# Sparse attention and a gated MLP on one core: scores on row halves, selection by added mask matmuls, and an engine order written out as a table

## The chip, the cores and the metric

One core of one Trainium2 chip runs the whole program. The metric is the device time of one execution in microseconds (us), lower is better; the profile's span, from the first to the last instruction, lies a few microseconds below it. TensorE is called PE here, VectorE DVE, ScalarE ACT, GpSimd POOL, SyncE SP.

## What is computed

For 4 batches and 8 heads, with 768 positions and head size 64, every query may look at its 6 best chunks of 32 keys. The choice goes by an upper bound of the chunk's scores:

```python
k_min, k_max = min and max over each chunk of 32 keys        # 24 chunks
ub = sum(maximum(q * k_min, q * k_max))                      # a bound for each query and chunk
ub = where(query's chunk >= chunk, ub, -1e9)
sel = the 6 chunks with the largest ub
scores = where(sel and causal, q k^T / 8, -1e9)
x = softmax(scores) @ v                                      # heads side by side: 768 x 512 per batch
h = gelu(x @ w_in);  u, v = halves of h
v = layernorm(v) * g_ln;  v = w_sg @ v + b_sg                # a 768 x 768 matrix over the positions
out = x + (u * v) @ w_out
```

Queries of the first 192 positions have at most 6 chunks and need no choice; the bounds concern the other 576.

## The kernel before

The program is made as a list of operations, each with an engine, a cost, the data that it reads and writes, and a priority. `schedule` places them by a greedy list schedule at build time; each engine then runs its own list in order, and semaphores hold what crosses engines. `fill` puts idle matmuls on a zero tile (L463) into early gaps of PE. Operations marked `port` on DVE are kept, in that schedule, out of the time of POOL's operations. Loads go by SP with at most 4 in flight. PSUM has two score tiles of 128x1024 (PSC) and four tiles of 128x512 (PSG), of which two (slots 2 and 3) serve the MLP.

Work goes by pairs of heads (16 pairs, two heads on partitions 0 to 63 and 64 to 127), and the selection by two pairs together (8 groups):

- `kside`: PE transposes k in f32 (L540), DVE takes the minimum and maximum of each chunk out of PSUM (`W`, L546, L559), ACT copies k in bf16 to `KA` and `KB` (L551 for pairs 0 to 3, L555 after).
- `qside`: the same for q (L575), ACT evacuates it to `qT` (L580), DVE makes `rT`, its positive part (L584), POOL casts it to `QA` (L587, L589, L592). From pair 4 on, DMAs on SP move the second head's half to `KB` and `QB`.
- `select`: for each half of the 576 queries, 8 f32 matmuls of 64 rows x 32 columns (L613; each shows as two instructions), DVE transposes the result to `U` (L621), takes the 8 largest of 18 query blocks (L629), compares (`Dn`, L632), and transposes back: eight transposes of 32x576 straight into `QA` and `QB` for pairs 0 to 3 (L640), one into `Dt` and DMAs after that (L644).
- `head`: the score matmul of one head has the selection in its contraction. `KA` and `KB` hold 64 rows of k and 24 or 64 rows of chunk indicators, `QA` and `QB` hold q and the selection. So one head is 14 bf16 matmuls with 2688 columns in all (L677), in three PSC tiles of 1024, 1024 and 640 columns, each followed by one exp on ACT (L682). POOL zeroes the upper triangles (L686), 21 matmuls of 65 columns make the output (L696, L703), DVE normalizes it (L711, L713).
- `xtrans`: PE transposes x (L723), DVE evacuates it (L727). `wsg_trans` does the same for w_sg (L735, L739).
- `moe_h(b)`: 24 matmuls of 512 columns for v (L751), gelu, statistics (L758, L760), the root on POOL (L764), six normalizations on DVE (L767), and 32 matmuls of 384 columns for u (L777). `moe_g(b)`: 48 matmuls of 384 columns (L794), two DVE operations each for the gate (L801, L805), 24 matmuls of 512 columns (L814), the residual (L820), the store.

The weights come by DMAs on POOL's queue that cast on the way (L498, L503, L508), issued after heads 0 to 6.

Of the kernel before, what the change touches and what calls it, by code (L numbers as in the profile page):

```python
# [13 lines left out]
LAT = {"pe": 0.15, "act": 0.20, "dve": 0.12, "pool": 0.15, "sp": 0.05}  # L14
TABLE_SWITCH = 1.3
WINDOW = 4


class PsumTile:


    def __init__(self, cls, slots=None):
        self.cls = cls
        self.slots = slots
        self.left = 0
        self.slot = None
        self.end = 0.0
        self.ops = []
# [6 lines left out]
class PsumClass:  # L35
    def __init__(self, aps):
        self.aps = aps
        self.owner = [None] * len(aps)

    def tile(self, slots=None):  # L40
        return PsumTile(self, slots)


class Op:
    __slots__ = ("eng", "fn", "cost", "prio", "deps", "dma", "ps", "alloc", "table", "burst",
                 "start", "end", "pos", "waits", "inc", "count", "idx", "lane", "bulk", "port")


class Program:

# [3 lines left out]
    def __init__(self):  # L54
        self.ops = []
        self.writer = {}
        self.readers = {}
        self.dma_sems = {}
        self.base = 0.0

    def op(self, eng, fn, cost, reads=(), writes=(), ps=(), alloc=None, dma=None, table=None,
           burst=None, prio=None, lane=0, bulk=False, port=False):
        o = Op()
        o.bulk = bulk
        o.port = port or (eng == "pool" and dma is None)
        o.lane = lane
        o.idx = len(self.ops)
        o.eng, o.fn, o.cost, o.dma, o.table, o.burst = eng, fn, cost, dma, table, burst
        o.prio = (self.base if prio is None else prio) + 1e-4 * o.idx
        deps = {}  # L70
        ps = tuple(ps) + ((alloc,) if alloc is not None else ())
        o.ps, o.alloc = ps, alloc
        for t in ps:
            t.left += 1
            for x in reversed(t.ops):
                if x.eng != eng:
                    deps.setdefault(x.idx, False)
                    break
            t.ops.append(o)
        for r in reads:  # L80
            w = self.writer.get(r)
            if w is not None:
                deps[w] = True
        for r in writes:
            w = self.writer.get(r)
            if w is not None:
                deps[w] = True
            for x in self.readers.get(r, ()):
                deps.setdefault(x, False)
# [5 lines left out]
        if dma is not None:  # L95
            last = self.dma_sems.setdefault(dma, [])
            if last:
                deps[last[-1]] = True
            last.append(o.idx)
        o.deps = deps  # L100
# [3 lines left out]
    def schedule(self):  # L104
        ops = self.ops
        succ = [[] for _ in ops]
        ndep = [len(o.deps) for o in ops]
        alloc = {o.alloc: o for o in ops if o.alloc is not None}
        for o in ops:
            hold = set()  # L110
            for t in o.ps:
                a = alloc[t]
                if a is not o:
                    hold.update((d, a.idx) for d in o.deps if d < a.idx and d not in a.deps)
            for d, a in hold:
                if a not in succ[d]:
                    succ[d].append(a)
                    ndep[a] += 1
            for d in o.deps:
                succ[d].append(o.idx)  # L120
        ready = {e: [] for e in ENGINES}
        rt = [0.0] * len(ops)
        for o in ops:
            if ndep[o.idx] == 0:
                ready[o.eng].append(o.idx)
        free = {e: 0.0 for e in ENGINES}
        order = {e: [] for e in ENGINES}
        table = None
        burst_left = {}
        for o in ops:  # L130
            if o.burst is not None:
                burst_left[o.burst] = burst_left.get(o.burst, 0) + 1
        cur_burst = None
        pool_owner = {}

        def slot_for(t, now):
            best = None
            for i, own in enumerate(t.cls.owner):
                if t.slots is not None and i not in t.slots:
                    continue  # L140
                at = 0.0 if own is None else (own.end if own.left == 0 else None)
                if at is not None and (best is None or at < best[0]):
                    best = (at, i)
            return best

        n = 0
        dma_free = 0.0
        soft_free = 0.0
        flight = []
        held = {"pool": 0.0, "dve": 0.0}  # L150
        while n < len(ops):
            pick = None
            for e in ENGINES:
                cands = []
                for i in ready[e]:
                    o = ops[i]
                    t = max(rt[i], free[e])
                    if o.alloc is not None and o.alloc.slot is None:
                        s = slot_for(o.alloc, t)
                        if s is None:  # L160
                            continue
                        t = max(t, s[0] + 0.15)
                    if e == "act" and o.table is not None:
                        if cur_burst is not None and o.burst != cur_burst:
                            continue
                        if o.table != table:
                            t += 0.0
                    if o.port:
                        t = max(t, held["pool" if e == "dve" else "dve"])
                    if o.bulk and len(flight) >= WINDOW:  # L170
                        t = max(t, ops[flight[-WINDOW]].end)
                    cands.append((t, o.prio, i))
                if not cands:
                    continue
                tmin = min(c[0] for c in cands)
                best = min((c for c in cands if c[0] <= tmin + 0.02), key=lambda c: c[1])
                if pick is None or best[0] < pick[0]:
                    pick = (best[0], e, best[2])
            if pick is None:
                raise RuntimeError("no operation can be scheduled")  # L180
            t, e, i = pick
            o = ops[i]
            ready[e].remove(i)
            if o.alloc is not None and o.alloc.slot is None:
                at, s = slot_for(o.alloc, t)
                old = o.alloc.cls.owner[s]
                if old is not None:
                    for x in old.users:
                        o.deps.setdefault(x, False)
                o.alloc.slot = s  # L190
# [13 lines left out]
            if o.port:  # L204
                held[e] = t + cost
# [703 lines left out]
```

## Time and profile before

| | |
|---|---|
| time, median of 3 runs | 267.15 us (265.14 to 267.54) |
| span of the profiled execution | 262.9 us |
| mean granted clock of PE, as a share of 2.4 GHz | 0.968 |
| DVE, ACT, POOL busy | 197.7, 153.4, 76.9 us |
| HBM read, written | 24.77 MB, 6.29 MB |

The table of runs gives no time of its own for the profiled execution; 262.9 us of span stand 4.25 us below the median. A busy PE is not a PE at its peak: matmuls are pipelined, and the recorded time of a group goes on past the start of the next. How long a group holds PE is read from the start of the next one where nothing is waited for.

### The profile page before, as it was taken

The numbers are of one execution on the slowest core, as the hardware profiler recorded it, in microseconds if no ns is written. First come the engines' busy times: TensorE is split into PE (matmuls) and PEld (weight loads), VectorE is DVE, ScalarE is ACT, GpSimd is POOL, SyncE is SP. The second block draws the span as 40 slices with busy tenths as digits, with TensorE's granted clock in tenths as the row PEclk, the third lists the DMA queues.
The fourth block names the chain that finished last, engine by engine and source line by source line (L and its number), as shares of the span: only waits on it lengthen the run. The fifth ranks groups of instructions, "written<-read, shape, count | busy, mean of one in ns | idle before, by whom it ended". The sixth has DMA issues, their size and how long they took to land.

```text
span 262.9 us, 5801 instructions
## 1 busy us (share of the span) xinstructions
PE 225.0 (86%) x2242; PEld 140.2 (53%) x2258; DVE 197.7 (75%) x561; ACT 153.4 (58%) x232; POOL 76.9 (29%) x99
## 2 busy tenths in 40 slices
PE   8886488987996599998899899997998998689874
PEld 3444256665743378655555577566445765434431
DVE  6949579787558668989677988886588876467883
ACT  1444848977649545655784974658757645846000
POOL 3353728653201424222212433134210211202000
PEclk9999689999999569999999999999999999999999
DMA  7999999998999904856751443122101031100033
GB/s 167 201 225 202 205 221 197 235 227 175 199 209 160 212 19 109 228 132 182 163 122 43 100 100 135 51 95 55 38 6 24 2 122 58 64 0 0 0 123 120
DMA packets 84652, 32.39 MB, mean 123 GB/s; under 512 B 77232, under 2 KB 80912, under 8 KB 84624
## 3 DMA queue, kind: packets, MB, share of 16 engines
q1 hardware_dynamic: 82608, 29.26, 48.1%
q0 software_dynamic: 2016, 2.75, 6.4%
q8 instruction: 18, 0.29, 0.5%
q14 instruction: 10, 0.08, 0.1%
HBM read 24.77 MB, written 6.29 MB: 118 GB/s over the span
## 4 chain that ended last, share of the span: by engine, by line
PE 50%; DVE 32%; ACT 9%; issue 6%; POOL 1%; POOLq 1%
PE PSG L794 9%; PE PSG L814 8%; PE PSC L677 8%; PE PSG L613 7%; DVE W L546 5%; ACT E L682 5%; DVE vhat L767 5%; PE PSG L751 4%; PE PSG L696 4%; DVE vsT L801 3%; PE PSG L777 3%; DVE uT L805 3%; DVE m_1 L629 2%; DVE XS L713 2%; PE PSC L463 2%
## 5 line engine op out<-in xcount | busy, mean ns | idle before, releaser
L682 ACT ACTIVATE E<-PSC 128x1024 bf16<-128x1024 f32 (+1 forms) x96 | 84.5, 920 | 44.7 <-PE PSC L677 44.1
L686 POOL TENSOR_SCALAR_AFFINE_SELECT E<-E 128x768 bf16<-128x768 bf16 x32 | 28.5, 892 | 59.9 <-ACT E L682 59.6
L794 PE MATMUL PSG<-wsgT,vhat 128*128 128x384 bf16 x192 | 36.6, 335 | 4.9 <-DVE vhat L767 3.0
L546 DVE TENSOR_REDUCE W<-PSG 128x12 f32<-128x384 f32 x64 | 33.1, 543 | 7.5 <-PE PSG L540 7.3
L677 PE MATMUL PSC<-QB,KB 128*128 128x128 bf16 (+1 forms) x224 | 26.0, 253 | 2.7 <-ACT E L682 2.7
L677 PE MATMUL PSC<-QA,KA 88*128 88x128 bf16 (+1 forms) x224 | 24.8, 249 | 3.4 <-ACT E L682 2.6
L794 PEld LDWEIGHTS PSG<-wsgT,vhat 128*128 128x128 bf16 x192 | 18.3, 100 | 17.6 <-DVE vhat L767 3.0
L801 DVE SCALAR_TENSOR_TENSOR vsT<-PSG,glnT,bsgbc 128x384 f32<-128x384 f32 x32 | 19.7, 614 | 7.6 <-PE PSG L794 7.5
L814 PE MATMUL PSG<-woutb,uT 128*128 128x512 bf16 x88 | 21.8, 380 | 3.9 <-DVE uT L805 3.3
L777 PE MATMUL PSG<-xT,winb 128*128 128x384 bf16 x128 | 23.8, 327 | 0.4 <-DVE xT L727 0.3
L696 PE MATMUL PSG<-vx,E 128*128 128x65 bf16 x480 | 20.4, 195 | 4.1 <-ACT E L682 2.7
L696 PEld LDWEIGHTS PSG<-vx,E 128*128 128x128 bf16 x480 | 18.0, 99 | 10.0 <-ACT E L682 5.6
L751 PE MATMUL PSG<-winb,xT 128*128 128x512 bf16 x90 | 21.6, 379 | 1.3 <-DVE xT L727 0.9
L575 PE MATMUL PSG<-identF,qn 128*128 128x128 f32 x96 | 16.1, 283 | 6.7 <-ACT KB L551 3.6
L755 ACT ACTIVATE vgb<-PSG 128x512 f32<-128x512 f32 x24 | 14.1, 598 | 13.1 <-PE PSG L751 13.1
L820 DVE TENSOR_TENSOR osb<-PSG,XS 128x512 f32<-128x512 f32 x24 | 16.6, 691 | 6.4 <-PE PSG L814 5.9
L677 PEld LDWEIGHTS PSC<-QA,KA 88*128 88x128 bf16 x224 | 16.3, 99 | 9.5 <-ACT E L682 4.6
L580 ACT ACTIVATE qT<-PSG 128x384 f32<-128x384 f32 x32 | 15.5, 496 | 9.5 <-PE PSG L575 9.4
L782 ACT ACTIVATE uT<-PSG 128x384 bf16<-128x384 f32 x32 | 15.6, 490 | 9.1 <-PE PSG L777 8.8
L598 POOL CAST vx<-vn 128x768 bf16<-128x768 f32 x16 | 13.2, 830 | 24.1 <-PE PSG L703 19.2
L677 PEld LDWEIGHTS PSC<-QB,KB 128*128 128x128 bf16 x224 | 15.9, 100 | 7.8 <-ACT E L682 4.9
L758 DVE BATCH_NORM_STATS2 stats<-vgb 128x6 f32<-128x512 f32 x24 | 16.0, 681 | 4.7 <-ACT vgb L755 4.7
(69 smaller groups left out, 343.7 us busy)
## 6 DMA issues: line engine op xcount, KB each, us to landing
kn<-in_k_dram SPq DMA_DIRECT2D x32, 192.0 KB, 3.6
qn<-in_q_dram SPq DMA_DIRECT2D x32, 192.0 KB, 3.6
vn<-in_v_dram SPq DMA_DIRECT2D x32, 192.0 KB, 3.5
out_dram<-osb SPq DMA_DIRECT2D x24, 256.0 KB, 2.0
vgb<-in_moe_w_sg_dram POOLq DMA_DIRECT2D x6, 192.0 KB, 5.9
QB<-QA SPq DMA_DIRECT2D x12, 96.0 KB, 2.2
KB<-KA SPq DMA_DIRECT2D x12, 96.0 KB, 3.0
winb<-in_moe_w_in_dram POOLq DMA_DIRECT2D x4, 256.0 KB, 5.9
```

The lines of the kernel that those rows point to most:

```text
L546: P.op("dve", lambda d, t=t, m=m, op=op, hf=hf: d.tensor_reduce(W[w][:, m, 12 * hf:12 * hf + 12], t.ap()[:, 0:TG].rearrange("p (c x) -> p ...
L613: r = e.matmul(t.ap()[32 * j:32 * j + 32, 0:n], W[w][lo:lo + 64, m, :], rhs, start=(m == 0), stop=(m == 1), tile_position=(lo, 32 * j))
L677: r = e.matmul(t.ap()[:, o:o + n], kt_[rows, 128 * kb:128 * kb + 128], qt_[rows, q0:q0 + n], start=True, stop=True, skip_group_check=True)
L682: P.op("act", lambda e, t=t, c0=c0, c1=c1: e.activation(E[es][:, c0:c1], t.ap()[:, 0:c1 - c0], ACTF.Exp, scale=SCALE), act(c1 - c0), reads ...
L686: P.op("pool", lambda g: g.affine_select(ev, ev, pattern=[[0, NT], [1, 128]], compare_op=ALU.is_ge, fill=0.0, base=0, channel_multiplier=- ...
L696: r = e.matmul(t.ap()[:, 65 * qb:65 * qb + 65], E[es][:, a:a + 128], vx[w][:, kb, i, :], start=first, stop=False, skip_group_check=True)
L751: r = e.matmul(t.ap()[:, 0:F], xT[s][:, dk, 128 * qt:128 * qt + 128], winb[:, dk, F:DFF], start=(dk == 0), stop=(dk == NDK - 1))
L777: r = e.matmul(t.ap()[:, 0:TG], winb[:, dk, 128 * fb:128 * fb + 128], xT[s][:, dk, TG * tg:TG * tg + TG], start=(dk == 0), stop=(dk == NDK ...
L794: r = e.matmul(t.ap()[:, 0:TG], vhat[s][:, sb, 128 * fb:128 * fb + 128], wsgT[:, sb, TG * tg:TG * tg + TG], start=(sb == 0), stop=(sb == N ...
L801: P.op("dve", lambda d, t=t, fb=fb, tg=tg, vs=vs: d.scalar_tensor_tensor(vsT[vs][:], t.ap()[:, 0:TG], glnT[:, fb:fb + 1], bsgbc[:, TG * tg ...
L814: r = e.matmul(t.ap()[:, 0:DM], gT[s][:, fb, 128 * qt:128 * qt + 128], woutb[:, fb, :], start=(fb == 0), stop=(fb == NF - 1))
L820: P.op("dve", lambda d, t=t, qt=qt, os_=os_: d.tensor_tensor(osb[os_][:], t.ap()[:, 0:DM], XS[:, (b % 2) * NT + qt, :], op=ALU.add), dve(D ...
```

## The change

Almost every function is written anew. What it does:

- **Order.** `schedule` and `fill` are gone. A table holds, as numbers of operations, the order of each engine, the PSUM slot of every tile and the idle matmuls (11 and a first one; before they are 44). There is no `port` any more.
- **Scores.** `scores(p)` takes both heads of a pair. Each piece of k and q is two matmuls with 64 rows each, one on partitions 0 to 63, one on 64 to 127, into two banks of a PSC tile; then the selection is added by further pairs of 64-row matmuls of `IND` with `Dt`. For a pair these are 2 x 14 matmuls with 2 x 2688 columns and 2 x 17 with 2 x 2432, in 6 operations, each with one exp of 2x512 (the sixth 2x128). `KB`, `QB` and their DMAs are gone.
- **Selection.** Pairs 0 and 1 are groups of their own, the other 14 pairs go two by two (9 groups). For two pairs, 8 matmuls on eight tiles (two row halves, four column groups) for `qT`, 8 for `rT`, and 4 bf16 matmuls that add the causal mask. DVE makes three transposes to `U` where there were two (one of 128x288, two of 64x288), 18 maxima and one compare as before, and always one transpose to `Dt`, which has three buffers. The eight transposes of 32x576 are gone.
- **Weights.** Plain f32 DMAs on SP into tiles that are not yet in use, then 14 casts on POOL. They stand among the loads of pairs 3 to 5.
- **Small.** x is evacuated by ACT instead of DVE. The MLP of the last batch uses all four PSG tiles, the others slots 2 and 3. w_sg is transposed row by row.

In the table's PE order (numbers put into names), the 96 score operations stand in 52 runs: 40 of two, 10 of one, 2 of three. 15 of these runs come ahead of the first MLP matmul. Ahead of that matmul stand also the transposes of pairs 0 to 5, four of the nine bounds, the eight heads of batch 0 and all of w_sg's transposes. The MLP of batch 0 then goes: 6 v operations and 8 u operations, with transposes, two score operations and one bound among them, then w_sg's product. After the last score operation come, of batch 2, two products with w_sg and four with w_out, then batch 3.

```diff
-    def schedule(self):
...
+    def place(self, order, slots):
+        ops = self.ops
+        self.order = {e: order[e] for e in ENGINES}
+        for t, s in zip(self.tiles, slots):
+            t.slot = s
...
-                def ub(e, t=t, hf=hf):
-                    for m in range(2):
-                        for j in range(4):
-                            w, lo = (2 * g + j // 2) % 4, 64 * (j % 2)
-                            rhs = qT[w][lo:lo + 64, LO + n * hf:LO + n * hf + n] if m == 0 else \
-                                rT[w][lo:lo + 64, n * hf:n * hf + n]
-                            r = e.matmul(t.ap()[32 * j:32 * j + 32, 0:n], W[w][lo:lo + 64, m, :], rhs,
-                                         start=(m == 0), stop=(m == 1), tile_position=(lo, 32 * j))
+        def ub(e):
+            for m in range(3):
+                for i in range(2):
+                    for x in range(n):
+                        for hf in range(2):
+                            lo, c, w = 64 * i, 64 * (i ^ x) + 32 * hf, ws[x]
+                            if m < 2:
+                                lhs = W[w][lo:lo + 64, m, :]
+                                rhs = qT[w][lo:lo + 64, LO + NH * hf:LO + NH * hf + NH] if m == 0 else \
+                                    rT[w][lo:lo + 64, NH * hf:NH * hf + NH]
+                            elif hf == 0:
+                                lhs, rhs = CMw[lo:lo + 64, :], CMb[lo:lo + 64, :]
+                            else:
+                                continue
+                            r = e.matmul(ts[x].ap()[c:c + 32, 0:NH], lhs, rhs, start=(m == 0), stop=(m == 2 - hf),
+                                         tile_position=(lo, c))
...
-            if 2 * g < DIRECT:
-                for j in range(4):
-                    w = (2 * g + j // 2) % 4
-                    qt_, lo = (QA[w], 64) if j % 2 == 0 else (QB[w], 0)
-                    P.op("dve", lambda d, j=j, qt_=qt_, lo=lo: d.transpose(
-                        qt_[lo:lo + 32, LO:S], Dn[u][32 * j:32 * j + 32].rearrange("p b c -> p (b c)")),
...
-                def sc(e, t=t, mms=mms):
-                    for (o, n, kb, q0) in mms:
-                        r = e.matmul(t.ap()[:, o:o + n], kt_[rows, 128 * kb:128 * kb + 128],
-                                     qt_[rows, q0:q0 + n], start=True, stop=True, skip_group_check=True)
+            def sc(e, t=t, mms=mms, masks=masks):
+                for x, (o, n, kb, q0) in enumerate(mms):
+                    for i in range(2):
+                        r = e.matmul(t.ap()[:, 512 * i + o:512 * i + o + n],
+                                     KA[w][64 * i:64 * i + 64, 128 * kb:128 * kb + 128],
+                                     QA[w][64 * i:64 * i + 64, q0:q0 + n], start=(x == 0), stop=False,
+                                     skip_group_check=True)
+                for x, (o, n, kb, hf, q0) in enumerate(masks):
+                    for i in range(2):
+                        r = e.matmul(t.ap()[:, 512 * i + o:512 * i + o + n],
+                                     IND[64 * i:64 * i + 64, hf, 128 * kb:128 * kb + 128],
+                                     Dt[u][64 * i:64 * i + 64, ux, q0:q0 + n], start=False, stop=(x == len(masks) - 1),
+                                     skip_group_check=True)
...
-                    P.op("pool", lambda g, i=i: g.dma_start(
-                        winb[:, i, :], bass.AP(w_in.tensor, 128 * DFF * i, [[DFF, 128], [1, DFF]])), 2.0,
+        load(dst, bass.AP(w_in.tensor, 128 * DFF * i, [[DFF, 128], [1, DFF]]), ("wi", i), names, 1400)
+        cast(winb[:, i, :], dst, DFF, ("wic", i), names, [("winb", i)])
...
-            P.op("dve", lambda d: d.tensor_copy(xT[b % 2][:, dk, :], t.ap(BF16)[:, 0:S]), dve(S, "ps", 2),
+        evac(XEV[b], lambda: xT[b % 2][:, dk, :], lambda: t.ap(BF16)[:, 0:S], S, ("xev", b, dk), [t],
...
-                t = ps_g.tile((2, 3))
+                t = ps_g.tile((2, 3) if b < B - 1 else None)
```

## Rows read from the trace of the kernel before

**Rows 1.** The page's part 1: busy time of each engine, its share, instructions.
```profile
PE 225.0 (86%) x2242; PEld 140.2 (53%) x2258; DVE 197.7 (75%) x561; ACT 153.4 (58%) x232; POOL 76.9 (29%) x99
```

**Rows 2.** Busy time by stretch, then granted clock, DMA share, GB/s.
```profile
0.00:23.10 23.10, 18.38 (x112) 9.47 (x114) 17.16 (x63) 8.19 (x16) 8.25 (x19) 1.00 0.90 193
23.10:64.36 41.26, 31.94 (x425) 22.03 (x425) 32.85 (x103) 30.18 (x48) 24.75 (x34) 0.92 1.09 211
...
84.30:90.00 5.70, 2.42 (x16) 1.35 (x14) 4.27 (x6) 4.76 (x7) 4.18 (x4) 0.64 0.91 178
90.00:228.60 138.60, 128.28 (x1384) 84.29 (x1394) 107.68 (x300) 88.47 (x126) 36.42 (x39) 0.98 0.35 91
228.60:262.90 34.30, 25.81 (x153) 11.87 (x155) 22.24 (x44) 8.76 (x15) 1.32 (x1) 1.00 0.12 47
```

**Rows 3.** The chain that ended last, in order: start, us, what.
```profile
11.11 0.99 DVE rT L584
...
16.47 2.19 PE PSG L613 x32
18.68 0.49 DVE U L621
19.20 1.47 DVE m_0 L629 x18
...
22.28 0.77 DVE QA L640
...
64.37 1.47 PE PSG L777 x8
...
90.20 2.10 PE PSG L794 x6
...
98.20 0.98 PE PSG L794 x6
```

**Rows 4.** Timeline of PE, 66 to 75 us: start, us, line, count.
```profile
65.79 0.38 PE L575 MATMUL PSG<-identF,qn 128*128 128x128 f32 x2
66.01 1.05 PE L677 MATMUL PSC<-QA,KA 88*128 88x128 bf16 x11
66.89 0.50 PE L735 MATMUL PSG<-identB,vgb 128*128 128x128 bf16 x6
67.23 1.46 PE L777 MATMUL PSG<-xT,winb 128*128 128x384 bf16 x8
68.53 0.83 PE L735 MATMUL PSG<-identB,vgb 128*128 128x128 bf16 x12
...
72.36 0.81 PE L777 MATMUL PSG<-xT,winb 128*128 128x384 bf16 x4
73.11 0.69 PE L613 MATMUL PSG<-qT,W 64*32 64x288 f32 x8
73.62 0.67 PE L613 MATMUL PSG<-rT,W 64*32 64x288 f32 x8
74.21 1.04 PE L751 MATMUL PSG<-winb,xT 128*128 128x512 bf16 x4
```

**Rows 5.** Groups by line and shape over the span: count, busy, mean ns.
```profile
L682 ACT ACTIVATE E<-PSC 128x1024 bf16<-128x1024 f32 x64 | 64.8, 1026 | 34.1 <-PE PSC L677 33.5
...
L682 ACT ACTIVATE E<-PSC 128x640 bf16<-128x640 f32 x32 | 22.6, 706 | 10.5 <-PE PSC L677 10.5
...
L727 DVE COPY xT<-PSG 128x768 bf16<-128x768 bf16 x16 | 8.9, 554 | 4.4 <-PE PSG L723 3.9
```

**Rows 6.** Timeline of all engines, 9 to 13 us.
```profile
9.44 0.49 ACT L580 ACTIVATE qT<-PSG 128x384 f32<-128x384 f32 x1
9.48 0.35 DVE L491 COPY KA<-IND 64x768 bf16<-64x768 bf16 x1
...
10.00 0.89 POOL L587 CAST QA<-qT 64x768 bf16<-64x768 f32 x1 [3.11 <-ACT qT L580]
10.22 0.88 DVE L491 COPY KA<-IND 64x768 bf16<-64x768 bf16 x1
```

More of the change, by code (lines that the diff above doesn't have):

```diff
@@ L37, in __init__ @@
         self.aps = aps
-        self.owner = [None] * len(aps)
+        self.tiles = []
     def tile(self, slots=None):
-        return PsumTile(self, slots)
+        t = PsumTile(self, tuple(range(len(self.aps))) if slots is None else tuple(slots))
+        self.tiles.append(t)
+        return t
 class Op:
-    __slots__ = ("eng", "fn", "cost", "prio", "deps", "dma", "ps", "alloc", "table", "burst",
-                 "start", "end", "pos", "waits", "inc", "count", "idx", "lane", "bulk", "port")
+    __slots__ = ("idx", "eng", "fn", "occ", "dur", "tag", "deps", "dma", "ps", "alloc", "table", "burst",
+                 "pos", "waits", "inc", "count", "xfer", "mode")
 class Program:
@@ L256, in link @@
                 ops[i].count = 16 * (j + 1)
-        last = None
-        for i in self.order["pool"]:
-            if last is not None and last.dma is None and (last.lane or ops[i].lane):
-                ops[i].deps[last.idx] = True
-            last = ops[i]
         know = [None] * len(ops)
@@ L274, in link @@
         while n < len(ops):
+            before = n
             for e in ENGINES:
@@ L294, in link @@
                     kn = dict(st)
-                    kn[proc(o)] = max(kn.get(proc(o), 0), place(o))
-                    if o.dma is None:
-                        pass
+                    kn[proc(o)] = max(kn.get(proc(o), 0), at(o))
                     know[o.idx] = kn
                     done[o.idx] = 1
+                    when[o.idx] = n
                     ptr[e] += 1
                     n += 1
+            if n == before:
+                raise RuntimeError("the order cannot run")
         for o in ops:
@@ new lines, in _build, with loads, prep @@
+    SEL, GRP, u = {}, {}, 0
+    for g in GROUPS:
+        for x, p in enumerate(g):
+            SEL[p] = (u % 3, x)
+        GRP[g[-1]] = (g, u % 2, u % 3)
+        u += 1
+    def loads(p):
+        if p < NP:
+            load_rows(p, "kn", k, kn)
+            load_rows(p, "qn", q, qn)
+    def prep(p):
+        kside(p)
+        qside(p)
+        vside(p)
+        if p in GRP:
+            select(*GRP[p])
+    loads(0)
+    loads(1)
+    load_v(0)
+    loads(2)
+    load_v(1)
+    prep(0)
@@ new lines, in _build @@
+    loads(3)
+    win_load(0)
+    win_load(1)
+    load_v(2)
+    win_load(2)
+    win_load(3)
+    prep(1)
+    small_loads()
+    prep(2)
+    load_v(3)
+    loads(4)
+    load_v(4)
+    for j in range(NT):
+        wsg_load(j)
+    prep(3)
+    loads(5)
+    for j in range(NF):
+        wout_load(j)
+    for p in range(4, NP + 4):
+        r = p - 4
+        scores(r)
+        for i in range(2):
+            head(r, i)
+        if p < NP:
+            prep(p)
+            loads(p + 2)
+            if p + 1 < NP:
+                load_v(p + 1)
+        xtrans(r // 4, r % 4)
+        if r == 3:
+            for tb in range(NT):
+                wsg_trans(tb)
+        if r % 4 == 3:
+            moe_h(r // 4)
+            moe_g(r // 4)
```

1070 lines of the change are left out of this document (480 added, 590 removed), and 55 rows, old and new, of the table TABLE.

## Prediction

> **What bounds the kernel now.** Read the busy shares first, then the stretches, then the chain. PE is busy 86% of the span, DVE 75%, ACT 58% [rows 1]; so PE is the candidate, but the share hides three kinds of time, which the stretches part [rows 2]. Up to 23.1 us no score has run: most of PE's 18.4 busy us there are idle matmuls on a zero tile. From 23.1 to 64.4 us, when the MLP's first matmul starts [rows 3], PE is busy 31.9 of 41.3 us, DVE 32.9, ACT 30.2, and the DMA share is full at 211 GB/s: nothing is used to the end, the stages wait for each other. From 90 to 228.6 us PE is busy 128.3 of 138.6 us (93%) and DVE 107.7: here PE is the bound, and work added to PE lengthens the kernel. At the end, from 228.6 us, PE is busy 25.8 of 34.3 us, since the last batch has nothing beside it. Between 84.3 and 90 us PE is busy 2.4 of 5.7 us at a granted clock of 0.64: it waits for the normalization, at half the clock of 2.4 GHz, and even at 90.2 us the six matmuls of w_sg's product take 2.10 us where others take 0.98 [rows 3].
>
> So the change is worth what it takes out of the start, that stall and the end, plus or minus the PE work of the long middle, one for one. I sum those four.
>
> **The start.** First scores before come at 23.1 us. The chain there is the bounds at 16.47 us (2.19 us), a transpose to U (0.49), the maxima (1.47), the compare, a transpose of 0.77 into QA [rows 3]; and the bounds of the first group wait for two pairs. But q of the first pair is out of PSUM at 9.44 + 0.49 = 9.93 us [rows 6]. With pair 0 alone, from there: positive part 0.5, bounds half of 2.19 and at most all of it if the clock is low, so 1.1 to 2.2, U 0.49, maxima 0.74, compare and transpose at half width 0.4 each, and some 0.6 of handing over: 4.2 to 5.3 us, so scores at 14 to 15 us, 8 to 9 us earlier. DVE also loses the eight transposes of 0.77 (6.2 us) and most of the copies of 0.35 that lie ahead of them, and gains one 0.49 transpose in each group of two pairs.
>
> What is late next? ACT, from 14 us on: for four pairs 20 exps of 1.03 and four short ones of some 0.4 (by the slope between the exps of 1024 and 640 columns [rows 5]), together 22 us; 17 evacuations of q and k at 0.49 [rows 6], 8 us; and four of x, 768 columns, between 0.71 and 1.03 by the same two exps, 3.2 us. These 34 us end at 48 us. The other limit is the loads, because w_sg's transposes stand ahead of the MLP in PE's order. Ahead of the last of its six blocks SP has 30 loads of 0.197 MB, w_in's 2.1 MB, the bias 0.39 and w_sg's 2.36: 10.7 MB. At 193 to 211 GB/s [rows 2] that is 51 to 55 us. The stores of the last stretch, with longer rows, moved 47 GB/s at a share of 0.12, as much as 390 at a full one; at that rate the 4.9 MB of weights take 12.4 us, and all is in at about 42 us. I take 50 us for the first MLP matmul instead of 64.4, since most of the weights have long rows but share the queue: **-14 us** (-9 to -18). By then PE has done one thing more (w_sg, 36 transposes, 2.0 us at 0.34 for six) and some 7 groups of transposes less (0.33 each, 2.3 us): even.
>
> **The stall.** From 84.3 to 92 us PE loses 3.3 us of waiting, and about 2 us by the half clock (2.10 instead of 0.98, and the same again on what runs from 84.3). The new order puts between batch 0's last v operation and w_sg's product five u operations (0.65 each, from 67.23 to 68.53 for two [rows 4]), two score operations, two transposes and a bound, by the paces below 3.3 + 1.1 + 0.7 + 1.3 = 6.4 us, where from the end of the v operations to w_sg's product the root, six normalizations and what DVE has among them take some 5 us (an estimate: the wait of 90.2 - 84.3 us, less one meeting of DVE and POOL). I take **-4 us**; at worst it comes back with the same 5 us.
>
> **The middle, PE's work.** The paces are start to start [rows 4]. Eleven score matmuls with 2048 columns hold PE from 66.01 to 66.89 us, 0.88 us, so a pair of 5376 columns takes 2.31 us. After the change a pair has 5120 columns in each row half. If the two halves run beside each other that is 2.20 us, or 2.5 if each of the 62 weight loads holds up its short matmul. Over the 12 pairs after batch 0: -1.3 to +2.3, I take 0. Does anything show that tiles run together? Two f32 transposes of 128 columns hold PE from 65.79 to 66.01 us, 0.86 ns a column. In the bounds, eight f32 instructions of 288 columns pass from 73.11 to 73.62 us; at that pace one after another they would need 1.98 us, so about four run at a time, two in each row half. But those lie in four different column groups; two row halves over the same columns are shown by no row.
>
> A bound of one half group holds PE from the end of the u operation before it (72.36 + 0.65 = 73.01) to 74.21 us: 1.20 us, of which 0.10 before the first and 0.08 after the last is not matmul but the change of tile shape. A group of two pairs is 2.40 us now. With eight tiles it is two rounds of 0.49 and a short bf16 one (288 columns, 0.12), with two changes some 1.3 us: 5 groups by -1.1 is -5.5 us. If eight tiles pass no faster than four it is 2.2, which makes it -1.
>
> Against this, every run of score operations now also changes the tile shape twice, at 0.10 each. After the first MLP matmul 37 runs stand in the table: +7.4 us. This cost has no cover, since PE is the bound there; were the runs single, 72 of them, it would be 14. The sum of the middle is **+2 us** (-3 to +7).
>
> Beside PE: x's evacuation leaves DVE (16 x 0.55 us) for ACT, and 14 casts (0.8 to 1.1 us each by POOL's cast of 768 columns at 0.89 [rows 6]) come to POOL, which is busy 29%. I cost both at nothing in the middle, ACT and POOL having over 40% idle; without that cover ACT's part would be 9 us. The SBUF copies by DMA that go (KB, QB, selection) lie on no step of the chain: nothing. The exps keep count and width. Three Dt buffers cost nothing.
>
> **The end.** Before, from 228.6 us on, PE has 8.5 us without work. The new order saves four products with w_out (2048 columns, 0.88 each) and one with w_sg (0.98) of batch 2 for the gaps there, 4.5 us that leave the full middle, and the last batch has four PSG tiles instead of two. DVE with its two gate operations still sets the pace of the last products. I take **-4 us** (-2 to -6).
>
> **Sum.** -14 - 4 + 2 - 4 = -20: the span goes from 262.9 to about 243 us. The profiled execution has no time of its own beside its span; the median lies 4.25 us above it, and I add that: **247 us**. With every term at its better end (-18, -4, -3, -6) it is 236 us, at its worse (-9, +1, +7, -2) 264.
>
> **Rivals.** *A: the two halves of a score do not run together.* Then a pair needs 2 x 5120 columns, 4.40 us instead of 2.20, and 16 pairs cost 35 us on the engine that bounds the middle; the start shifts too, but ACT's 32 us there hides some 9 of them. So 247 + 26 to 35, about 275 us: slower than before. It decides where a pair takes 2.20 + 20/16 = 3.45 us, 1.3 at a time instead of 2: there the 20 us gained are used up. For it: no row shows two halves over the same columns. Against it: the bounds, whose two row halves overlap now. I give 0.10.
>
> *B: they run together only in part.* The pieces of up to 128 columns may be too short for two weight loads each, and pass one after another: they are 21 of the 31 in a pair, with 2304 columns, 0.99 us more at the pace of 0.88 for 2048. 16 pairs make 16 us, of which ACT hides 4 in the start: 259 us. Chance 0.10. TensorE: Matmul & The Clock Gate (the Trainium skill, Part 3, Measured speedup vs the span model) gives 3.07 times for four row tiles; three quarters of the ideal would be an estimate of 2.9 us a pair, 11 us in all and 258 us; no run here shows it.
>
> On the new bounds the four at a time of [rows 4] decide: both row halves write one PSUM tile there. TensorEngine Tiling (Array Packing) (the Trainium skill, Restrictions and Gotchas, Gotcha 1) says that different row tiles cannot use one PSUM bank at the same time; by it each round of the new bounds would be two and its -5.5 would be -1. The trace does not agree.
>
> *C: the wait moves instead of going.* The greedy order reacts to its own cost model; the table is just as fixed. It has no rule that keeps DVE's fast operations out of POOL's time. What that costs is seen at 10.22 us: the copy that takes 0.35 us takes 0.88 while POOL casts from 10.00 on [rows 6]. Some 97 such operations on DVE, POOL busy 30% of the span, 0.5 us for each meeting: 15 us on DVE at most, of which perhaps half reaches PE, with the stall of 5 us back: 247 + 7 + 5 = 259 us. Chance 0.17.
>
> *D: more is gained.* If the table also removes half of what PE lacks between 90 and 228.6 us (10.3 us unbusy there), and the loads reach the 42 us: 247 - 5 - 6 = 236, and with the end fully packed 232. Chance 0.13.
>
> **How the numbers follow.** The forecast (240 to 255) has 0.45, A 0.10, B 0.10, C 0.17, D 0.13; 0.05 is left for no change by sums I do not see. The point is the forecast's 247. The range 232 to 263 holds the forecast, D's inner part, B and most of C, and leaves out A and the rest: about 0.8. A measurement of this kernel tells about 1% from no change, 2.7 us. Faster than 264.5: forecast, D, B and nearly all of C, 0.82. Within 1%: 0.06. Slower: A and a little of the rest, 0.12.
>
> **What the new profile would show.** First score at 14 to 15 us, first MLP matmul at about 50. Two score operations of 512 columns holding PE some 0.9 us together with a following gap of 0.1; 1.8 us would be rival A. A bound of two pairs in 1.1 us. No half clock between 60 and 95 us. PE busy over 93% in the middle, and fewer than 8 idle us after the last score. Wrong would be: a first MLP matmul after 58 us (loads or w_sg's casts on POOL late), PE waiting on DVE operations that last twice their time, or a half clock in the first 20 us, where only 11 idle matmuls are left, that outlasts the first scores.

## The result and the profile after

The changed kernel takes 234.57 us (median of 4 runs, 234.19 to 235.71) against 267.13 us: ratio 0.8793, 95% interval 0.8751 to 0.8836. That is 32.6 us less, where the sum said 20. Its profiled execution has a span of 234.0 us.

The page of the kernel after, part 1 and the clock line of part 2, beside [rows 1]:

```profile
PE 210.6 (90%) x2783; PEld 136.3 (58%) x2800; DVE 189.3 (81%) x530; ACT 159.1 (68%) x240; POOL 76.0 (32%) x98
...
PEclk9999999999999999999999999999999999999999
```

The busy time by stretch of the kernel after (columns as in [rows 2]); the last row runs from the first MLP matmul to the end, 197.8 us is the end of the last exp:

```profile
0.00:14.76 14.76, 9.27 (x53) 5.75 (x55) 10.80 (x37) 4.39 (x8) 6.41 (x19) 1.00 0.99 192
14.76:55.93 41.17, 32.62 (x615) 23.45 (x615) 29.18 (x84) 31.21 (x46) 25.25 (x31) 1.00 0.92 249
55.93:92.00 36.07, 33.51 (x367) 20.83 (x368) 33.02 (x102) 25.50 (x44) 10.08 (x12) 1.00 0.79 173
92.00:197.80 105.80, 104.07 (x1551) 69.34 (x1555) 89.29 (x255) 86.01 (x124) 32.35 (x38) 1.00 0.34 90
...
55.93:234.00 178.07, 168.71 (x2120) 107.14 (x2132) 149.29 (x410) 123.50 (x187) 44.33 (x50) 1.00 0.40 104
```

The kernel before: the stall with the half clock behind it, the long middle from there to the last exp, and in the last row all from the first MLP matmul to the end:

```profile
84.30:96.00 11.70, 8.21 (x59) 5.53 (x58) 7.19 (x12) 5.94 (x9) 4.18 (x4) 0.57 0.72 134
96.00:227.90 131.90, 122.48 (x1343) 80.11 (x1351) 104.75 (x293) 86.61 (x124) 36.42 (x39) 1.00 0.34 91
...
64.37:262.90 198.53, 174.66 (x1705) 108.68 (x1719) 147.66 (x397) 115.04 (x170) 43.87 (x46) 0.97 0.40 97
```

The first score comes at 14.76 us (23.1 before [rows 2]), the first MLP matmul at 55.93 (64.37 [rows 3]). So 8.4 us are gained ahead of it and 20.5 behind it. Of those 20.5, PE's busy time gives 174.66 - 168.71 = 6.0; the time in which PE is not busy falls from 23.9 to 9.4 and gives 14.5. Between 92 and 197.8 us PE is busy 98% of the time, where it was 93% in the long middle of before [rows 2].

In the chain that ended last, 30 us of the kernel after are loads one behind the other, with a single cast on POOL among them:

```profile
33.64 5.07 DMA qn<-in_q_dram
38.72 4.00 DMA uT<-in_moe_w_sg_dram
...
43.70 5.10 DMA uT<-in_moe_w_sg_dram
48.81 2.79 DMA qn<-in_q_dram
...
55.63 4.24 DMA qn<-in_q_dram
59.89 3.67 DMA kn<-in_k_dram
...
63.65 0.85 PE PSG L445 x6
```

The timeline of PE shows a bound of two pairs (L510) ahead of the first MLP matmul (L699), and around batch 0's normalization scores (L566, L572), a further bound and the first product with w_sg (L716):

```profile
54.67 0.72 PE L510 MATMUL PSG<-qT,W 64*32 64x288 f32 x16 [0.56 <-DVE rT L478]
...
55.93 0.82 PE L699 MATMUL PSG<-xT,winb 128*128 128x384 bf16 x4
...
68.88 0.40 PE L566 MATMUL PSC<-QA,KA 64*128 64x128 bf16 x6
69.11 0.36 PE L572 MATMUL PSC<-Dt,IND 64*128 64x128 bf16 x6
69.31 0.38 PE L566 MATMUL PSC<-QA,KA 64*128 64x256 bf16 x4
69.52 0.38 PE L572 MATMUL PSC<-Dt,IND 64*128 64x256 bf16 x4
69.84 1.47 PE L699 MATMUL PSG<-xT,winb 128*128 128x384 bf16 x8
...
72.70 0.72 PE L510 MATMUL PSG<-qT,W 64*32 64x288 f32 x16
73.21 0.70 PE L510 MATMUL PSG<-rT,W 64*32 64x288 f32 x16
73.69 0.33 PE L510 MATMUL PSG<-CMb,CMw 64*32 64x288 bf16 x4
73.95 0.82 PE L699 MATMUL PSG<-xT,winb 128*128 128x384 bf16 x4
74.89 2.12 PE L716 MATMUL PSG<-wsgT,vhat 128*128 128x384 bf16 x12
```

The two score operations hold PE from 68.88 to 69.84 us, 0.96 us with the gap behind them; the bound holds it from 72.70 to 73.95, 1.25 us. Ahead of the product with w_sg PE has no wait to speak of (at most 0.3 us from the u operation's last matmul to 74.89), and the clock is full: the stall is gone.

To place gains and losses, every profile below is cut at the first and the last exp: ahead of the first exp the kernel prepares, between them scores and MLP share PE, behind the last only the MLP is left. The kernel before, cut so:

```profile
0.00:23.80 23.80, 19.08 (x122) 10.10 (x125) 17.86 (x63) 8.86 (x18) 8.25 (x19) 1.00 0.90 195
23.80:227.90 204.10, 180.10 (x1970) 118.23 (x1980) 157.58 (x455) 135.11 (x200) 67.29 (x79) 0.96 0.58 128
227.90:262.90 35.00, 25.81 (x153) 11.87 (x155) 22.24 (x44) 9.44 (x17) 1.32 (x1) 1.00 0.12 46
```

and the kernel after:

```profile
0.00:15.10 15.10, 9.61 (x61) 6.03 (x64) 11.14 (x38) 4.40 (x9) 6.64 (x19) 1.00 0.99 193
15.10:197.80 182.70, 169.85 (x2516) 113.34 (x2526) 151.15 (x440) 142.71 (x213) 67.45 (x78) 1.00 0.56 142
197.80:234.00 36.20, 31.13 (x212) 16.97 (x213) 26.98 (x55) 12.00 (x20) 1.90 (x2) 1.00 0.19 74
```

So -8.7 us up to the first exp, -21.4 between the exps, +1.2 behind the last, where PE now has 31.1 us of work instead of 25.8.

### The profile page after: what moved, and what is told of

It reads as the page before. It is cut to its first block, busy times and chain, and to the rows that moved or that the text cites. A ratio compares the mean times of both kernels' runs of the same rounds, so it can differ in the third digit from the quotient of the medians.

```text
span 234.0 us, 6773 instructions
## 1 busy us (share of the span) xinstructions
PE 210.6 (90%) x2783; PEld 136.3 (58%) x2800; DVE 189.3 (81%) x530; ACT 159.1 (68%) x240; POOL 76.0 (32%) x98
## 4 chain that ended last, share of the span: by engine, by line
PE 59%; DMA 14%; DVE 14%; ACT 7%; issue 3%; POOL 1%; SPq 0%; DVEq 0%; ACTq 0%; POOLq 0%
PE PSG L716 10%; PE PSC L566 7%; PE PSG L445 7%; PE PSG L736 7%; PE PSG L699 6%; ACT E L581 6%; PE PSG L670 6%; DMA qn<-in_q_dram 5%; PE PSC L572 5%; PE PSG L605 5%; DMA uT<-in_moe_w_sg_dram 4%; PE PSG L510 3%; DMA kn<-in_k_dram 3%; PE PSG L612 2%; DVE vsT L723 2%
## 5 line engine op out<-in xcount | busy, mean ns | idle before, releaser
L589 POOL TENSOR_SCALAR_AFFINE_SELECT E<-E 128x768 bf16<-128x768 bf16 x32 | 27.4, 877 | 45.5 <-ACT E L581 45.4
L566 PE MATMUL PSC<-QA,KA 64*128 64x128 bf16 (+2 forms) x448 | 34.3, 245 | 1.5 <-ACT E L581 1.1
L716 PE MATMUL PSG<-wsgT,vhat 128*128 128x384 bf16 x192 | 34.8, 326 | 0.1
L572 PE MATMUL PSC<-Dt,IND 64*128 64x128 bf16 (+6 forms) x544 | 31.7, 222 | 0.0
L480 POOL CAST QA<-qT 128x768 bf16<-128x768 f32 x16 | 14.7, 916 | 36.1 <-PE PSC L572 19.4
L699 PE MATMUL PSG<-xT,winb 128*128 128x384 bf16 x128 | 24.7, 327 | 0.4 <-DVE vsT L723 0.2
L716 PEld LDWEIGHTS PSG<-wsgT,vhat 128*128 128x128 bf16 x192 | 17.9, 98 | 12.1 <-DVE vhat L688 0.5
L736 PE MATMUL PSG<-woutb,uT 128*128 128x512 bf16 x84 | 21.4, 379 | 1.7 <-issue 0.8
L572 PEld LDWEIGHTS PSC<-Dt,IND 64*128 64x128 bf16 x544 | 20.2, 94 | 3.1
L566 PEld LDWEIGHTS PSC<-QA,KA 64*128 64x128 bf16 x448 | 14.2, 94 | 13.1 <-issue 5.0
L485 POOL CAST vx<-vn 128x768 bf16<-128x768 f32 x16 | 13.2, 827 | 25.8 <-DMA vn<-in_v_dram 17.8
L461 ACT ACTIVATE KA<-PSG 128x384 bf16<-128x384 f32 x32 | 15.7, 498 | 8.5 <-DVE W L457 8.2
L474 ACT ACTIVATE qT<-PSG 128x384 f32<-128x384 f32 x32 | 15.2, 498 | 8.7 <-PE PSG L445 8.5
L445 PE MATMUL PSG<-identF,kn 128*128 128x128 f32 x96 | 16.4, 293 | 4.3 <-DMA kn<-in_k_dram 4.0
L605 PE MATMUL PSG<-vx,E 128*128 128x65 bf16 x480 | 19.1, 194 | 1.2 <-ACT E L581 1.2
```

The source lines that it names most:

```text
L445: r = e.matmul(t.ap()[:, 128 * j:128 * j + 128], src[:, 3 * hf + j].rearrange("p i d -> p (i d)"), identF[:], is_transpose=True)
L566: r = e.matmul(t.ap()[:, 512 * i + o:512 * i + o + n], KA[w][64 * i:64 * i + 64, 128 * kb:128 * kb + 128], QA[w][64 * i:64 * i + 64, q0:q0 ...
L572: r = e.matmul(t.ap()[:, 512 * i + o:512 * i + o + n], IND[64 * i:64 * i + 64, hf, 128 * kb:128 * kb + 128], Dt[u][64 * i:64 * i + 64, ux, ...
L589: P.op("pool", lambda g, ev=ev: g.affine_select(ev, ev, pattern=[[0, NT], [1, 128]], compare_op=ALU.is_ge, fill=0.0, base=0, channel_multi ...
L605: r = e.matmul(t.ap()[:, 65 * qb:65 * qb + 65], E[es][:, i, a:a + 128], vx[w][:, kb, i, :], start=first, stop=False, skip_group_check=True)
L699: r = e.matmul(t.ap()[:, 0:TG], winb[:, dk, 128 * fb:128 * fb + 128], xT[s][:, dk, TG * tg:TG * tg + TG], start=(dk == 0), stop=(dk == NDK ...
```

## The experiments

The theories: either the order makes the gain (the table fills the gaps of the middle, and the operations hardly matter), or the operations do (shorter bounds, row halves, x off DVE). Apart from e5 and e12, each kernel is the one after with the named thing changed. Ratios are to the kernel before, with 95% intervals.

**e1_greedy: the new operations under the old rule.** All orders, slots and idle matmuls (23) are what the rule of the kernel before chooses for the new operations; its score operations stand in 64 runs, the table's in 52.

```diff
 TABLE = {
     "pe": (
-        "1 44 48 55 53 83 79 60 90 88 184 180 102 95 176 106 113 182 ...
+        "1 44 48 53 55 79 83 60 88 90 95 102 106 174 111 113 176 178 ...
```

> All operations of the changed kernel, but the order, the PSUM slots and the idle matmuls come from the greedy list schedule of the kernel before (its rule, its kind of priorities, DVE's fast operations kept out of POOL's time). Theory 1, the order: most of the gain of the middle is the table's, so this takes 248 to 256 us. Theory 2, the operations (shorter bounds, x off DVE, row halves): the order matters little and this takes 235 to 241 us.

Measured: 267.06 us, ratio 0.9992 (0.9949 to 1.0035). Both expectations fail: under this rule the new operations are worth nothing. The profiled execution took 268.85 us, 1.8 more than the median, so up to that much of the rows below is its own. By stretch:

```profile
0.00:17.40 17.40, 14.37 (x106) 7.85 (x108) 13.50 (x46) 4.83 (x10) 7.00 (x20) 1.00 1.13 197
17.40:230.10 212.70, 181.81 (x2519) 118.16 (x2530) 154.87 (x441) 145.59 (x214) 69.28 (x78) 0.97 0.50 124
230.10:267.10 37.00, 27.66 (x174) 14.83 (x176) 22.31 (x45) 10.02 (x18) 1.32 (x1) 0.91 0.11 43
```

The start still gains 6.4 us, so that gain belongs to the operations. The middle is 30 us longer than after's with the same instructions: 12.0 us more of PE's busy time and 18.0 in which PE does nothing. About half of the 12.0 is the clock (an estimate: a mean of 0.97 instead of 1.00 over 212.7 us is at most 6.4). What PE waits for most in e1 from 24 to 198 us (total us, times, longest):

```profile
PE PSC L566 <- ACT E L581: 9.2, 15, 2.6
```

and in the kernel after, same window:

```profile
PE PSG L445 <- DMA kn<-in_k_dram: 3.2, 3, 1.4
...
PE PSC L566 <- ACT E L581: 0.7, 2, 0.4
```

Under the old rule PE waits 15 times for an exp to free a score tile; in the table it waits twice. In e1's timeline 10 of the 15 waits, 5.7 us, come straight behind another score operation. The 9.2 us are half of the 18.0; the longest of the other waits are for POOL and DVE (2.6 and 2.4 us).

**e5_old_ops_new_order: the old operations in a searched order.** The kernel before and its operations, with the rule replaced by a table of its own, found by a search as after's was. An operation also waits for all earlier users of its PSUM slot, as a fixed order needs.

```diff
-        P.schedule()
+        P.place({e: [int(x) for x in TABLE[e].split()] for e in ENGINES}, [int(c) for c in TABLE["slots"]],
...
                     deps.setdefault(x.idx, False)
-                    break
+                    continue
```

> The kernel before's own operations (whole score matmuls, bounds of one pair in four tiles, x evacuated by VectorE, two buffers for the transposed selection), but the order of every engine, the PSUM slots and 25 idle matmuls come from a table that was searched for, as after's was. With e1 (new operations, old rule: 267.06 us, nothing gained) it completes the square of operations and order. Theory 1, the order alone makes the gain: 231 to 241 us, at most 6 us above after. Theory 2, the gain needs both, because only the shorter operations leave the order something to fill: 248 to 262 us. Between 241 and 248: the operations are worth some of it under a good order.

Measured: 252.12 us, ratio 0.9459 (0.9413 to 0.9505), inside the 248 to 262 us of theory 2: the order alone gains 15 us, the whole gain needs both. That shorter operations leave the order more to fill, theory 2's reason, is not shown by the time alone. By stretch:

```profile
0.00:21.30 21.30, 15.55 (x102) 8.22 (x103) 15.39 (x56) 8.68 (x18) 8.61 (x18) 1.00 1.15 201
21.30:209.10 187.80, 170.91 (x1945) 114.26 (x1943) 162.16 (x451) 134.86 (x200) 66.44 (x81) 0.98 0.61 133
209.10:249.20 40.10, 33.98 (x197) 15.09 (x195) 29.24 (x57) 9.45 (x17) 1.40 (x2) 0.98 0.21 79
```

This completes the square (medians, us; the old rule with the old operations is the kernel before):

| | old rule | searched order |
|---|---|---|
| old operations | 267.1 | 252.1 |
| new operations | 267.1 | 234.6 |

With the old operations the order takes 16.3 us from the middle, of which 5.1 come back behind the last exp, where PE now has 34.0 us of work instead of 25.8; with the new ones it takes 30.0, and nothing comes back (36.2 us behind the last exp against e1's 37.0). The operations are worth nothing under the old rule and 17.5 us under a searched order; of the spans' 15.2 us, 6.2 lie ahead of the first exp, 5.1 between the exps and 3.9 behind them. A part of the 5.1 is seen in e5's chain: the copies into QA and KB, which the new operations don't have, and a late v load behind them on SP's queue:

```profile
140.31 2.22 DMA QA<-Dt
...
147.76 2.98 DMA KB<-KA
154.12 3.34 DMA vn<-in_v_dram
```

**e12_old_ops_four_slots: e5 with after's four slots for the last batch.**

```diff
-                t = ps_g.tile((2, 3))
+                t = ps_g.tile((2, 3) if b < B - 1 else None)
```

> e5 (the kernel before's operations in a searched order, 252.12 us) with one part of after's added: the last batch's MLP may use four PSUM slots instead of two. e11 took the four slots from after and lost 6 us (240.73 us); in e5 the stretch behind the last exponential is 40.1 us long, in after 36.2. If the four slots are what the old operations lack at the end: 246 to 249 us. If the end of e5 is held by something else, VectorE above all: 251 to 253 us.

Measured: 251.79 us, ratio 0.9448 (0.9374 to 0.9521): as e5. The slots are not what the old operations lack at the end, when the order was searched without them.

**e11_last_batch_two_slots: the reverse, after without them.**

```diff
-            t = ps_g.tile((2, 3) if b < B - 1 else None)
+            t = ps_g.tile((2, 3))
```

> After, with the last batch's MLP on two PSUM slots instead of four (the order of every engine stays). The sum of the prediction had -4 us at the end, from the four slots and from more work drawn ahead. If the slots are what keeps TensorE going in the last 34 us (29.16 us busy): 237 to 242 us. If the order alone does it, with two slots always free in time: 234 to 236 us.

Measured: 240.73 us, ratio 0.9022 (0.8979 to 0.9064), 6 us above after. Of its span of 238.2 us the stretch behind the last exp has grown from 36.2 to 41.9 us; the others are as in after:

```profile
196.30:238.20 41.90, 32.80 (x212) 15.64 (x212) 27.23 (x54) 12.08 (x20) 1.83 (x2) 1.00 0.17 64
```

PE's waits in e11 from 197 us to the end, of which after has only the fourth, 0.4 us:

```profile
PE PSG L736 <- ACT uT L704: 1.4, 2, 0.8
PE PSG L670 <- ACT vgb L674: 1.2, 1, 1.2
PE PSG L699 <- DVE osb L743: 1.1, 1, 1.1
PE PSG L736 <- DVE uT L727: 0.4, 1, 0.4
```

An order that was found for four slots loses 6 us with two; one found for two gains nothing from four (e12). Order and slots belong together.

**e6_split_runs: 35 runs of two score operations taken apart.**

```diff
 TABLE = {
     "pe": (
-        "1 44 48 55 53 83 79 60 90 88 184 180 102 95 176 106 113 182 111 174 178 138 ...
+        "1 44 48 55 53 83 79 60 90 88 184 102 180 95 176 106 113 182 111 174 138 178 ...
```

> After, with 35 of its runs of two score operations on TensorE taken apart: the next operation on TensorE goes between the two, so that the tile shape changes 70 times more (64 rows to 128 rows and back). Nothing else is moved. If a change of shape costs 0.10 us of TensorE's time, as the sum of the prediction took it, and nothing covers it, +7 us: 240 to 243 us. If it is covered, or the array takes the next shape without draining, within 1 us of after: 233 to 236 us.

Measured: 244.35 us, ratio 0.9178 (0.9141 to 0.9215). The middle:

```profile
14.90:206.20 191.30, 178.13 (x2527) 112.79 (x2528) 152.00 (x441) 143.77 (x213) 66.27 (x77) 1.00 0.56 136
```

It is 8.6 us longer, 8.3 of it PE's busy time. The score operations stand in 84 runs, 32 more than in after: in three places the operation that was split off joins the next run. So 64 changes of tile shape were added, not 70, and each costs 0.13 us that nothing covers. The table's longer runs are thus part of why its order is better: e1's 12 runs more are 24 changes, some 3.2 us of its 30 (an estimate at that price).

**e2_halves_apart: all matmuls of one row half, then all of the other.**

```diff
-                for x, (o, n, kb, q0) in enumerate(mms):
-                    for i in range(2):
+                for i in range(2):
+                    for x, (o, n, kb, q0) in enumerate(mms):
...
-                for x, (o, n, kb, hf, q0) in enumerate(masks):
-                    for i in range(2):
+                    for x, (o, n, kb, hf, q0) in enumerate(masks):
```

> The matmuls of a score operation are issued half by half: all of the first row half, then all of the second, instead of in turns. Theory 1 says that the table works since PE is full, so PE's extra time shows one for one: if the halves overlap only when they stand in turns, 16 pairs cost 2.1 us each, 34 us less what the start hides, so 258 to 268 us. Rival: the halves never overlapped and the gain is all from elsewhere, then 234 to 236 us.

Measured: 241.3 us, ratio 0.9073 (0.9043 to 0.9104), between the cases. The timeline of e2 at the same two operations:

```profile
67.67 0.41 PE L566 MATMUL PSC<-QA,KA 64*128 64x128 bf16 x5
...
68.76 1.48 PE L698 MATMUL PSG<-xT,winb 128*128 128x384 bf16 x8
```

They hold PE from 67.67 to 68.76, 1.09 us instead of 0.96: 0.13 for each two, 6.2 for 96, nearly the whole loss of 6.7. So the halves overlap in great part even when they are queued half by half; one after another they would need twice the time.

**e3_four_tiles: the bounds of the two pairs one after the other, four tiles at a time.**

```diff
-            for m in range(3):
-                for i in range(2):
-                    for x in range(n):
+            for x in range(n):
+                for m in range(3):
+                    for i in range(2):
```

> The bounds of two pairs go pair by pair, so that four tiles run at a time instead of eight. Theory 1: seven groups of two pairs cost 1.1 us more each, of which some five lie in the full middle: 239 to 242 us. Theory 2: the same or more, since the selection behind it is late too. Rival: eight tiles pass no faster than four, then 234 to 236 us.

Measured: 235.35 us, ratio 0.8858 (0.8827 to 0.8889), at most a little slower. The time is the rival's, its reason is not: in the trace the same bound passes from 72.12 to 73.63 us, 1.51 us instead of 1.25, which for seven such groups is 1.8 us at most. In that trace the second pair's matmuls start before the first pair's are done.

**e4_x_on_dve: x evacuated by VectorE again.**

```diff
-    XEV = ("act", "act", "act", "act")
+    XEV = ("dve", "dve", "dve", "dve")
```

> x is evacuated by DVE again, as before the change, at the place in DVE's order where its transposes are done. 16 operations of 0.55 us go from ACT (0.82 each) to DVE. Theory 1: neither engine is the bound in the middle, 234 to 237 us. Theory 2, that a lighter DVE made the middle full: 238 to 243 us.

Measured: 233.13 us, ratio 0.877 (0.8719 to 0.8821): not slower. The move to ACT gave nothing.

**e7_six_in_flight, e8_wout_late: is it the loads that hold the start?**

```diff
# e7
-            if len(self.loads) >= bulk:
-                deps.add(self.loads[-bulk])
+            k = 6 if len(self.loads) < 60 else bulk
+            if len(self.loads) >= k:
+                deps.add(self.loads[-k])
# e8
-    for j in range(NF):
-        wout_load(j)
...
+            if p == 6:
+                for j in range(NF):
+                    wout_load(j)
```

> After, with up to six loads in flight instead of four for the first 60 loads. The chain of after is nothing but loads from 33.6 to 63.65 us, at 249 GB/s between 14.76 and 55.93 us with the 16 DMA engines busy 0.92 of the time. If the few loads in flight limit it: the loads end 3 to 4 us earlier and so does the kernel, 230 to 232 us. If the DMA engines do (0.92 busy already): 234 to 236 us, no change.

> After, with the eight loads of w_out and their casts moved behind the loads of the last pair of heads, where the selection that reads them has still not come. 2 MB less is ahead of the first MLP matmul's data and of the last pairs' q, k and v. If the loads bound the start, 8 us of loads at 249 GB/s leave the stretch, and what waits next (the scores' own work on TensorE) takes part of it: 229 to 232 us. If the loads only look late, since the order holds the work until then anyway: 234 to 236 us. If w_out then comes too late for the first output matmuls: slower, 236 to 240 us.

Measured: e7 232.32 us, ratio 0.8722 (0.8676 to 0.8768); e8 235.12 us, ratio 0.8815 (0.8763 to 0.8867). More loads in flight may give 2 us (the intervals overlap), fewer bytes ahead give nothing. Neither moves the first MLP matmul much: 54.44 us in e7, 54.74 in e8, 55.93 in after. In e8 loads of later pairs, and one of w_out, still stand in the chain up to 76 us.

**e10_no_idle_matmuls.**

```diff
-    "filler": (
-        "55:3 83:3 184:5 "),
+    "filler": "",
```

> After without its 11 idle matmuls, nothing else changed. They run before the first score. Theory 1, an order in which TensorE never waits long keeps the clock by itself: the clock stays at full level after the first scores, 234 to 236 us. Rival, the idle matmuls keep the clock up in the start, which the loads bound: some 10 us of the start at half clock, on a stretch in which TensorE was 62% busy, 236 to 240 us.

Measured: 233.8 us, ratio 0.8758 (0.8714 to 0.8802), no loss. The mean granted clock is 0.96 in the stretch that the loads bound, and back at 1.00 behind it:

```profile
14.80:55.90 41.10, 33.66 (x602) 24.21 (x601) 26.53 (x83) 31.41 (x45) 24.77 (x30) 0.96 0.97 250
55.90:76.00 20.10, 18.26 (x150) 10.48 (x151) 18.70 (x58) 12.49 (x25) 5.88 (x7) 1.00 1.05 212
```

**e9_x_dve_six_in_flight: e4 and e7 together.** Its diff is theirs.

> After with the two edits together that measured a little below it: x evacuated by VectorE again (e4, 233.13 us) and up to six loads in flight for the first 60 loads (e7, 232.32 us). If they are independent: 0.877 and 0.8722 against after's 0.8793 are 0.0023 and 0.0071, so a ratio near 0.870, 230 to 232 us. If both only shorten the same stretch, which the loads bound: 232 to 233.5 us.

Measured: 230.59 us, ratio 0.8649 (0.8614 to 0.8685). This is faster than after, too: its interval lies below after's. It is what two independent gains would give, or a little more.

## Why the prediction held, and where its sum was off

**The start: direction right, -14 was too much.** The first score came where the sum had it, at 14.76 us; e1 has it at 16.81, so most of this gain is the new operations'. The loads were in between the sum's two bounds, 42 and 51 to 55 us: w_sg's last block landed at 48.80, at a mean of 230 GB/s from the start. But the first MLP matmul came at 55.93, not at 50: -8.4 us. What the step left out lies between. The q load that follows that block in the chain landed at 51.60, and its transposes, its evacuation, its positive part and the bound from 54.67 us on stand ahead of the MLP in PE's order. The sum let the stretch end with the loads and called PE's other work there "even".

**The stall: right, and worth more.** From 76 us on PE works without the 5.7 us at clock 0.64 [rows 2], and the operations that were to stand ahead of w_sg's product stand there. What went is 3.5 us of waiting from 84.3 to 96 us and about 3.7 of half clock (an estimate: the level was half from 86 to 96 us, PE was busy 7.5 us of these, and half of that is the price), 7.2 where the sum took 4.

**The middle: the term that was off.** "The sum of the middle is +2" added up PE's work alone and took the time in which PE does nothing as given; only rival D let the table remove half of it, with 0.13. Its single prices were good: a bound 1.25 us (forecast 1.3), two score operations 0.96 with their gap (0.9 and 0.1), a change of shape 0.13 (0.10, e6). What the sum left out is the order. Stall, middle and end were to give 6 us behind the first MLP matmul and gave 20.5. With 7.2 for the stall and 4.1 for PE's gaps behind the last exp, 9.2 us remain that the middle gained, where the sum had it lose 2: PE has 6.9 us less without work and 2.3 less of busy time. e1 and e5 show that the order is what removes such time: the same operations under the old rule have 18.0 us more of it between the exps than the table, and the old operations in a searched order have 7.1 us less of it than before (204.10 - 180.10 against 187.80 - 170.91); the other 9.2 of e5's 16.3 are PE's work, most of it moved behind the last exp. The text had argued that the table is just as fixed as the greedy order; but in the greedy order PE waits 9.2 us for exps where the table lets it wait 0.7.

**The number: partly luck.** 234.57 us lies inside the stated range through rival D, not through the forecast's 240 to 255. Two errors worked against each other: the start gave 5.6 us less than its term, what follows gave 14.5 more. A third went the same way as the second: the 4.25 us that were added to the span stand at 0.57 here (median 234.57, span 234.0), and in the profiled execution of after itself time and span lie 1.71 apart.

**The end: PE's gaps went, as forecast.** Behind the last exp PE is unbusy 5.1 us of 36.2 instead of 9.2 of 35.0. The four slots carry that (e11: 6 us), though only in an order made for them (e12).

**The rivals.** A and B are out: an operation's two halves of 960 columns pass in 0.43 us (68.88 to 69.31), as long as one half's columns take at the pace of 0.88 us for 2048 [rows 4]. The estimate of 2.9 us a pair from the Trainium skill's 3.07 times for four row tiles (TensorE: Matmul & The Clock Gate, Part 3, Measured speedup vs the span model) is too dear here: at this pace a pair's 5120 columns take 2.3. The new bounds, too, do not agree with Gotcha 1 of TensorEngine Tiling (Array Packing) in the Trainium skill, by which different row tiles cannot use one PSUM bank at the same time. Sixteen f32 instructions (eight matmuls) of 288 columns, with both row halves in the same two PSUM tiles but in different column groups, pass in 0.51 us (72.70 to 73.21). One after another, at 0.86 ns a column [rows 4], they would take 3.96, so nearly eight run at a time, and eight are both row halves at once. C did not come: PE's waits for DVE from 24 to 198 us are 2.6 us in all. D's mechanism came, larger than D priced it, and without its loads, which were in at 48.80 us and not at 42.

**What was costed at nothing.** x on ACT is worth nothing, as forecast (e4), and the idle matmuls of the start are not needed (e10).

**What stays open.** Why the new operations give 17.5 us under a searched order, and which of them: no run changes the weights' path, the bounds or the row halves alone under an order searched for it. The 6.2 us of the start are theirs under either rule (6.4 in e1); the 5.1 of the middle are in part the DMA copies, shown in one place only; the 3.9 at the end are not the slots alone. The 2.3 us of PE's busy time, where the sum had 2 more, are not accounted for either. And each corner of the square is one order: a better one might take more from the old operations than e5 does, and a greedy rule with other priorities might leave the new ones less than e1 loses.

## What to carry to other kernels

When an order is replaced, price it: cut the trace into stretches and count the time in which the bounding engine does nothing as something that an order can win, not as a constant. Operations and order can need each other: here new operations under the old rule gave nothing, the order alone 15 us, both 32.6. So try a change of operations again after the order is searched anew, and search the order for the slots it will have.

## What the runs showed of the hardware

Two row halves of TensorE overlap almost as well when their matmuls are queued half by half as when they alternate: 1.09 us for 0.96 (e2). A change of tile shape costs 0.13 us of TensorE, uncovered (e6). For the same tile of 128x768, ACT took 824 ns (after) and DVE 554 [rows 5], and yet nothing was lost or gained by a measurable amount in moving it (e4). Idle matmuls in the start did not hold TensorE's clock later, and after does not need them. Before, with 44 of them, the mean granted clock was 0.97: it was half from about 28 to 35 us, after PE had been busy 0.8 us between 25 and 28, and from 86 to 96 us, after 1.5 us between 82 and 86. In after, with 11 and a first one, the mean was 1.00; in e10, with the first one alone, it was 0.99, half from 31 to about 35 us, after PE had been busy 1.2 us between 28 and 31.
